# H3 and MLP in two layers: taps packed with k, unit-wise rows for k, v and filter, 39 idle matmuls for 52, and another order list

## The chip, the cores and the metric

The kernel runs on one core of a Trainium2 chip. The metric is the time of one execution on the device in microseconds (us). TensorE (PE) multiplies matrices, VectorE (DVE) and ScalarE (ACT) work element by element, GpSimd (POOL) does little here, and SyncE (SP) issues most DMA transfers; ScalarE issues a few at the start.

## The reference

`x` has 2048 rows of 640 numbers. Two layers are applied twice, A, B, A, B, each on a layer norm of x and added to x:

```python
def A(q, k, v, shift_k, ssm_k, ssm_D):      # q = layernorm(x)
    k_shift = causal_conv(k, shift_k)        # 4 taps a channel
    kv = k_shift * v
    y = long_causal_conv(kv, ssm_k)          # filter as long as the sequence, by FFT
    return q * (y + kv * ssm_D)

def B(x, w1, w2):                            # x = layernorm(x)
    return relu(x @ w1) @ w2                 # 640 -> 1728 -> 640
```

k, v, taps, filter and D are the same in both A layers, so the long convolution is computed once.

## The kernel before

**Tiling.** The 2048 rows are cut into 8 chunks of 256 (`NC`), the 640 channels into 5 tiles of 128 (`NDT`). The long convolution works by units: a unit is one or two (chunk, channel tile) pairs. Chunks 0 and 1 have the units (c,0)+(c,1), (c,2)+(c,3) and (c,4) each; from chunk 2 on most units pair two chunks of one tile. A unit passes through `transform` (L447 on): its k is shifted and scaled by the four taps and summed into `acc` (ScalarE or VectorE), multiplied by v, folded into `sd`; TensorE transposes `sd` into `pt`, ScalarE copies that to `sh`, and TensorE multiplies it by the matrices cM into `pr`, the spectrum `at`. The filter `hf` (for chunk 0 with D added to its first row, L494) is multiplied by the matrices cG and cX into `pg`, the spectrum `gt`. `products` multiplies spectra of all pairs of chunks that meet, sums them on VectorE and turns them back on TensorE (`pq`, with cM). The MLP (`main`) multiplies in float16 in a high and a low part, w1 first (tile `h`), then w2 (tile `o`); its weights `ws` are loaded and split on the chip.

**Order.** Every piece of work is recorded as an operation of one engine, with what it reads and writes (`Plan.op`). The operations are then issued in an order that is written out by hand into the file as text: `ORDER` decodes to 16-bit numbers, each the place of an operation in the order of recording. Every engine executes its own operations in that order, and waits at the first whose inputs aren't there. A buffer of a ring is reused once its last reader is done.

**Start.** 42 idle matmuls (`spin`, L1585, 128x128, identity by identity, read by nobody) are recorded before the first unit and 10 more (L1605) that wait for the first unit's `pg` (6) or `pt` (4). The names in `ACTQ` are fetched on ScalarE's queue: dD, shs (the taps, 10 KB), cG, cX, cM; all else on SyncE's. In the order list ScalarE's start is dD, shs, cG, cX, a first activation (L384), the activation of k's second half (L538), cM. SyncE's is hf, the two pieces of the first unit's k (L471), v, then k, v and hf of the second unit. The first unit multiplies k's first half by taps on VectorE (L540, L545) and starts its second half on ScalarE (L538). On TensorE the list has 42 idle matmuls, four pg operations of the first unit, 6 idle, pt, 4 idle, three pg operations of the second unit, two pr, a pg. A pg operation of a unit of two pairs is four records of 256 columns in the trace.

**Layout.** k, v and the filter lie in memory as [channel tile, chunk, 128 channels, columns] with 262 or 256 float32 columns, so a unit of two pairs is loaded in two rows of 1 KB a partition (`pieces`, L417). The lines that the change touches: `NSPIN`, `NLONG`, `NMORE`, `NLAST` and `ACTQ` (L40), `pieces` (L417), the loads in `transform` (L463 to L475), the first unit's taps (L533 to L547).

Of the kernel before, what the change touches and what calls it, by code (L numbers as in the profile page):

```python
# [18 lines left out]
ALU = mybir.AluOpType  # L19
# [20 lines left out]
NSPIN, NLONG, NMORE, NLAST = 30, 12, 6, 4  # L40
ACTQ = ("cG", "dD", "shs", "cX", "cM")
# [32 lines left out]
    "kO7hbXab7@zX5#$zyWCj!2!Yne*%00W&)A|YXYnSKmx-7)d8*oX9C0l*a2(;#R2*O`vGbK*#U3@`~h(SfCAb9Z30#S{Q-Ugi~`&N"
    "-T`s~+X4Oo;{bsI00NBybOHealmg!Y;Q^5X;sIp<f&$$E;{o6Sa{{megaQHrZUX250|EpB<pJUVbpq)DvI2zy<pKo)Zvy54=K+%f"
    "<N=QY{{e#nh63&Z1_J5<^8l{`cLJ3HkOFoB2LcHK>j9er3Ic}$3j&D(hyw2c@B#4wmI9Xom;wv}>;Z}bz5?w5@&TO!tpc0^=K?hZ"
    "2m-+Zu>$h}nF6x{^Z}j%ngX8!paS&)4FaPAqyiHHr2-BDv;xEep#l#A5CZlA#R9bgrvmo@5dyaY_yM>AK>`v26auCKwgR~V83M)v"
    "LIM>6r~*R*76PdP8Uh~z^8&g8#{$3tL;^SjMFJZFM*^Y(7XrKjAOiIQIt0Q3$O69t=mNU}$pX^?NCHU$7y?QHAp$-G3Ix3ZO9J--"
    "90J1v)B@H5$^y#*B?8w1%mPdT<^m!D=>qBk9Rk$?>;fJF4FvcC*aA%gC;}-0P68$ZCj!v|%>p9=*#h(eECMY8Py#Lj(gJt_Q3Cb?"
    ">jEzV+5-6kFapj3H3BvQ`T{Wm3<OdF?E=pN?gIM)`~o=yI|Tm%+XDRpHUuOB&;r~7?*j1xDgrA4GXgRK76UW_4g?PbIRZBXHv$j@"  # L80
    "{sI64cLW0iQvx~y1OpNT@B#q?7X#e_-U2uR5d=I00s|NW1q0v$6$BFmP6Xcq;Q}KBc?1RnsscL#83XbH2LluY;sQMc7z7#v76d#3"
    "Jpvm8PXr4D7X%~(CIou~J^~p88U!2z9Rno<Cj=q`2m?U`2?HYoKLiQ`8w4N&9s?f(Ap;}>C<7@2<N_Q7OaxE_B?B%4Ap|A^3j-$u"
    "3<DwrF#{b0C<H(RG6M|*LIf%U4g)I$D+7E4F9UuALj*+xDFj9YDg+(`QUrPgQv^5zIRhUAO$1Z~4+D4vFat&cIs-ccECVeAAOtl7"
    "HUmTie+1(KHv=;RGy_otR|H1{J_A(*Rs<3QECekCJOe!gE(8z*KLUaTPXb5;NdsC0Nd#L2KLdmW6ax_hSOlB|69Y;FF9a|ISp-}J"
    "fCNGVN&{sCKm#!ZW(2DOXarpZO9M;;UIbqRnFM_VV+271Lj#)xO#?CnO9W&Dp9F;jp#*~jL<2<wfdo$jPy=TKX#{Nq%miQrP6HJK"
# [36 lines left out]
    "o(dxg?+AGcBnc=9DG4SCTMF<9QVQ`1@(5iDehQrmR0>=QObK2JO$jdvp9-J~P6<y5p$aMqcM2y7#tKjgQ3;|7D+zrHe+pF!EeXjA"
    "dkRtsED2KyR0*RBd<x47Rti`NE(tLSRS8)MG6_}*R|$a%GYOaqS_yy(qzW_%f(rTyUkWz~H3>EeUI|<Yg9?NSFbP`;stQ*M&I(-#"
# [1616 lines left out]
```

## Time and profile before

| | us |
|---|---|
| median of 3 runs | 837.17 |
| lowest and highest | 836.2, 837.32 |
| the profiled execution | 835.64 |
| its span, first to last instruction | 833.9 |
| TensorE busy in it | 828.1 |
| VectorE busy | 776.0 |
| ScalarE busy | 603.7 |

The span is a little shorter than the execution's time, which has a start and an end around it. Times in the trace count from the span's start. PE is a matmul, PEld the load of its weights, which runs beside the matmul before it. A matmul of float32 operands stands in the trace as two records.

### The profile page before, as it was taken

How to read it: one execution, taken by the hardware profiler on the slowest of the kernel's cores; microseconds unless marked ns; L12 is line 12 of the kernel's file. 1: busy time of each engine (PE TensorE's matmuls, PEld its weight loads, DVE VectorE, ACT ScalarE, POOL GpSimd, SP SyncE). 2: the span in 40 equal slices, each digit the busy share in tenths (PEclk: the TensorE clock that was granted, in tenths of full speed). 3: DMA queues.
4: the chain of work that ended last, by engine and by line, in shares of the span. 5: the costliest groups of instructions: out<-in, count | busy, mean ns of one | idle time of the engine just before them, and what ended most of it. 6: DMA issues, size and time to landing. Idle time of an engine off the chain costs nothing.

```text
span 833.9 us, 20585 instructions
## 1 busy us (share of the span) xinstructions
PE 828.1 (99%) x8091; PEld 657.5 (79%) x8091; DVE 776.0 (93%) x1404; ACT 603.7 (72%) x1505; POOL 45.9 (6%) x58
## 2 busy tenths in 40 slices
PE   9999999999999999999999999999999999999998
PEld 8887878887877777777777777777767788888886
DVE  7999999999899999999999999999989799897776
ACT  5997798568997787868668675777736587868532
POOL 0000000000000121000110010111100000000000
PEclk9999999999999999999999999999999999999999
DMA  9978778978999886997997797788997465240300
GB/s 290 385 251 318 266 216 257 278 242 273 315 291 219 263 160 253 258 305 219 235 294 204 211 279 196 231 199 251 306 268 248 140 221 128 64 90 2 58 34 32
DMA packets 138435, 182.37 MB, mean 219 GB/s; under 512 B 53857, under 2 KB 95713, under 8 KB 138338
## 3 DMA queue, kind: packets, MB, share of 16 engines
q1 hardware_dynamic: 129296, 169.60, 65.4%
q0 software_dynamic: 8320, 10.49, 8.5%
q8 instruction: 63, 1.03, 0.5%
q10 hardware_dynamic: 722, 0.96, 0.4%
q14 instruction: 34, 0.28, 0.1%
HBM read 125.24 MB, written 34.08 MB: 191 GB/s over the span
## 4 chain that ended last, share of the span: by engine, by line
PE 99%; POOL 0%; DVE 0%; issue 0%; DVEq 0%; POOLq 0%
PE h L1340 10%; PE h L1343 10%; PE h L1341 10%; PE o L1258 10%; PE o L1313 9%; PE o L1312 9%; PE o L1315 8%; PE h L1328 4%; PE oc L1312 2%; PE oc L1313 2%; PE h L1330 2%; PE oc L1315 2%; PE pg L594 2%; PE hs L1373 2%; PE h L1373 2%; PE pq L816 1%
## 5 line engine op out<-in xcount | busy, mean ns | idle before, releaser
L1343 PE MATMUL h<-xT,w 128*128 128x256 f16 (+1 forms) x1000 | 229.0, 249 | 0.0
L1341 PE MATMUL h<-xT,w 128*128 128x256 f16 (+1 forms) x1000 | 229.0, 249 | 0.0
L1340 PE MATMUL h<-xT,w 128*128 128x256 f16 (+1 forms) x1000 | 229.0, 249 | 0.0
L1313 PE MATMUL o<-w,hh 128*128 128x512 f16 x336 | 127.3, 379 | 0.0
L1312 PE MATMUL o<-w,hh 128*128 128x512 f16 x336 | 127.3, 379 | 0.0
L775 DVE TENSOR_TENSOR pacc<-pacc,pd 128x1536 f32<-128x1536 f32 (+1 forms) x75 | 123.4, 1645 | 0.2
L1341 PEld LDWEIGHTS <-w 128*128 128x128 f16 x1100 | 107.6, 98 | 14.6
L1340 PEld LDWEIGHTS <-w 128*128 128x128 f16 x1100 | 107.6, 98 | 13.6
L1343 PEld LDWEIGHTS <-w 128*128 128x128 f16 x1000 | 97.8, 98 | 6.4
L1313 PEld LDWEIGHTS <-hh 128*128 128x128 f16 x672 | 65.7, 98 | 26.1
L1312 PEld LDWEIGHTS <-hh 128*128 128x128 f16 x672 | 65.7, 98 | 25.8
L770 DVE TENSOR_TENSOR pd<-Ax,Gx 128x768 f32<-128x768 f32 x83 | 78.6, 952 | 1.4 <-DMA Gx<-G 1.2
L1315 PE MATMUL o<-w,hl 128*128 128x512 f16 x208 | 78.8, 379 | 0.0
L1479 ACT ACTIVATE hh<-h 128x512 f16<-128x512 f32 (+1 forms) x97 | 46.7, 483 | 37.6 <-PE h L1328 12.7
L1313 PE MATMUL oc<-w,hh 128*128 128x128 f16 x336 | 73.5, 219 | 0.0
L1312 PE MATMUL oc<-w,hh 128*128 128x128 f16 x336 | 73.5, 219 | 0.0
L1315 PEld LDWEIGHTS <-hl 128*128 128x128 f16 x416 | 40.7, 98 | 24.5
L1328 PE MATMUL h<-xT,w 128*128 128x256 f16 (+1 forms) x400 | 57.8, 251 | 0.0
L1315 PE MATMUL oc<-w,hl 128*128 128x128 f16 x208 | 45.5, 219 | 0.0
L488 ACT ACTIVATE tp<-kt,shs 128x256 f32<-128x256 f32 (+1 forms) x78 | 43.2, 573 | 1.2 <-DVE acc L562 1.0
L770 DVE TENSOR_TENSOR pd<-at,Gx 128x768 f32<-128x768 f32 x46 | 43.1, 952 | 0.1
L1328 PEld LDWEIGHTS <-w 128*128 128x128 f16 x400 | 36.3, 98 | 5.4
(304 smaller groups left out, 2062.1 us busy)
## 6 DMA issues: line engine op xcount, KB each, us to landing
Ax<-A SPq DMA_DIRECT2D x89, 384.0 KB, 5.2
Gx<-G SPq DMA_DIRECT2D x89, 384.0 KB, 4.9
A<-at SPq DMA_DIRECT2D x14, 768.0 KB, 6.1
G<-gt SPq DMA_DIRECT2D x14, 768.0 KB, 6.7
ws<-in_w SPq DMA_DIRECT2D x28, 320.0 KB, 6.5
y<-Y SPq DMA_DIRECT2D x22, 320.0 KB, 4.8
x<-in_q SPq DMA_DIRECT2D x16, 320.0 KB, 4.2
gs<-in_hF SPq DMA_DIRECT2D x20, 256.0 KB, 4.5
```

Source lines behind the costliest of these rows:

```text
L488: ACT.activation(o[:, i : i + m], kview(i, m, j), AF.Copy, scale=shs[:, t, j : j + 1])
L770: ew(f"mac{j % POOLMOD}", 768, lambda e, x=dst[i], av=av, gv=gv: e.tensor_mul(x.t, av(), gv()), [ax, gx], [dst[i]], pr_)
L775: dve(768 * (hi - lo), lambda lo=lo, hi=hi, pd=pd: DVE.tensor_add(acc[:, lo:hi], acc[:, lo:hi], pd[:, lo:hi]), [*sums[lo:hi], *dst[lo:hi]] ...
L1258: PE.matmul(b[:, c : c + w], x, y[:, z : z + w], start=done[i] == 1, stop=end, skip_group_check=fin)
L1312: PE.matmul(z, hh[:, c], wh[:, d], start=(j == JS[0] and i == 0 and (h == 0 or s == S[0])), stop=False)
L1313: PE.matmul(z, hh[:, c], wl[:, d], start=False, stop=end and tail)
L1315: PE.matmul(z, hl[:, c], wh[:, d], start=False, stop=end)
L1328: PE.matmul(p[:, z], wh, xv(t, x), start=b and x == 0, stop=e and x == 1)
L1340: PE.matmul(p[:, z], wh, xv(t, 0), start=b, stop=False)
L1341: PE.matmul(p[:, z], wh, xv(t, 1), start=False, stop=tail and e)
L1343: PE.matmul(p[:, z], wl, xv(t, 0), start=False, stop=e)
L1479: act(2 * R, lambda pv_=pv_, hh=hh: ACT.activation(hh.t, pv_(), AF.Relu), [src], [hh], URGENT)
```

## The change

The taps no longer have a transfer of their own: the array for the first unit's k is 20 columns wider, and its first piece brings taps and k's first half in one DMA. The first unit reads its taps from there; GpSimd copies them to `shs` for the later units. k, v and filter are packed on the host by unit, [unit, 128, 2 x columns], so that a unit of two pairs is one row of 2 KB a partition. Idle matmuls: 34 + 5 in place of 42 + 10. The order list is another one. Decoded and matched to the operations, it starts so: on TensorE 27 idle matmuls, two pg of the first unit, 2 idle, a pg, 3 idle, a pg, 5 idle, pt, 2 idle, three pg of the second unit, two pr, a pg. On ScalarE: dD, cG, cX, the first activation, cM, L538. SyncE's first eight transfers keep their order.

```diff
-NSPIN, NLONG, NMORE, NLAST = 30, 12, 6, 4
-ACTQ = ("cG", "dD", "shs", "cX", "cM")
+NSPIN, NLONG, NMORE, NLAST = 30, 4, 3, 2
+ACTQ = ("cG", "dD", "cX", "cM")
+KW = 262
...
 ORDER = (
...
+SHW = 4 * NDT
...
-    fetch("shs", 80, lambda e: e.dma_start(shs.t, shk), [shs], soonest("shs"))
...
     def pieces(u, ap):
-        (c0, t0), n = u[0], len(u)
-        if n == 1:
-            return ap[t0, c0 : c0 + 1].rearrange("c p n -> p c n")
-        if u[1][1] == t0:
-            return ap[t0, c0 : c0 + 2].rearrange("c p n -> p c n")
-        return ap[t0 : t0 + 2, c0].rearrange("c p n -> p c n")
+        n, z = len(u), SHW if rank(u) == 0 and ap is kT else 0
+        wd = KW if ap is kT else 2 * P
+        return ap[rank(u), :, z : z + n * wd].rearrange("p (c n) -> p c n", n=wd)
...
-            x = R(k, [P, n, wd], k + nm)
+            if (u[0], k) != ((0, 0), "kt"):
+                x = R(k, [P, n, wd], k + nm)
             if u[0] == (0, 0) and k == "kt":
-                kts = [Sub(x, lambda t, i=i: t[:, i]) for i in range(n)]
-                for i in range(n):
-                    dma(4 * wd, lambda i=i: SP.dma_start(kts[i].t, src_kt(u[i])), [], [kts[i]], soonest("kt0_0" + "b" * i))
+                pl, tag, bufs, stream = ring[k]
+                raw = T(pl, tag, bufs, [P, SHW + n * KW], k + nm, stream=stream)
+                x = Sub(raw, lambda t: t[:, SHW:].rearrange("p (c n) -> p c n", n=KW))
+                kts = [Sub(raw, lambda t, i=i: t[:, SHW + i * KW : SHW + i * KW + KW]) for i in range(n)]
+                sh0 = Sub(raw, lambda t: t[:, 0:SHW].rearrange("p (t j) -> p t j", j=4))
+                for i, (z0, z1) in enumerate(((0, SHW + KW), (SHW + KW, SHW + 2 * KW))):
+                    dma(4 * (z1 - z0), lambda z0=z0, z1=z1: SP.dma_start(raw[:, z0:z1], kT[0, :, z0:z1]), [], [kts[i]] + [sh0] * (i == 0), soonest("kt0_0" + "b" * i))
+                plan.op("POOL", 0.2, lambda: POOL.tensor_copy(shs.t, sh0.t), [sh0], [shs], pr_)
...
-                    act(256, lambda i=i, t=t: ACT.activation(accs[i].t, kview(i, 1, 0), AF.Copy, scale=shs[:, t, 0:1]), [kts[i], shs, warm], [accs[i]], pr_, 0.09)
+                    act(256, lambda i=i, t=t: ACT.activation(accs[i].t, kview(i, 1, 0), AF.Copy, scale=sh0[:, t, 0:1]), [kts[i], sh0, warm], [accs[i]], pr_, 0.09)
...
+def _packed(x, more=0):
+    units, wd = _units(), x.shape[3]
+    r = np.zeros((len(units), P, 2 * wd + more), np.float32)
+    for k, u in enumerate(units):
+        for i, (c, t) in enumerate(u):
+            r[k, :, i * wd : i * wd + wd] = x[t, c]
+    return r
...
+    kT = _packed(dl(kl), SHW)
+    kT[0] = np.concatenate([f(A_shift_k).reshape(NDT, P, 4).transpose(1, 0, 2).reshape(P, SHW), kT[0, :, : 2 * KW]], 1)
...
-        "vT": dl(vl),
-        "shk": f(A_shift_k).reshape(NDT, P, 4).transpose(1, 0, 2),
-        "hF": hf.reshape(NDT, NC, P, 2 * P),
-        "hR": hr.reshape(NDT, NC, P, 2 * P),
+        "kT": kT,
+        "vT": _packed(dl(vl)),
+        "hF": _packed(hf.reshape(NDT, NC, P, 2 * P)),
+        "hR": _packed(hr.reshape(NDT, NC, P, 2 * P)),
```

## Rows read from the trace of the kernel before

**Rows 1.** Page, part 1: busy us (share of span), instructions by engine.

```profile
PE 828.1 (99%) x8091; PEld 657.5 (79%) x8091; DVE 776.0 (93%) x1404; ACT 603.7 (72%) x1505; POOL 45.9 (6%) x58
```

**Rows 2.** The page, part 4: the chain that ended last, by engine.

```profile
PE 99%; POOL 0%; DVE 0%; issue 0%; DVEq 0%; POOLq 0%
```

**Rows 3.** Waits of TensorE: who waited for whom, us in total, times, longest us.

```profile
PE spin L1585 <- POOL heps L368: 1.9, 1, 1.9
```

**Rows 4.** Windows: stretch, length, busy us by engine, clock, DMA share, GB/s.

```profile
4.00:6.00 2.00, 2.00 (x22) 2.00 (x20) 1.86 (x5) 0.16 (x1) 0.00 (x0) 1.00 0.95 275
...
20.00:200.00 180.00, 180.00 (x2061) 147.11 (x2060) 176.13 (x348) 141.81 (x357) 0.00 (x0) 1.00 0.86 282
```

**Rows 5.** Chain in order of time, 0 to 24: start us, us, what.

```profile
1.95 4.47 PE spin L1585 x42
6.42 3.51 PE pg L594 x16
9.93 0.34 PE spin L1605 x6
10.26 0.44 PE pt L650 x4
...
10.93 2.84 PE pg L594 x12
```

**Rows 6.** Instructions in order of time around 6 us.

```profile
6.25 0.43 PE L594 MATMUL pg<-hf,cG 128*128 128x256 f32 x1
```

**Rows 7.** ScalarE's queue in order of time; landing time of cG, issued at 1.71.

```profile
1.31 0.36 ACTq L379 DMA_DIRECT2D shs<-in_shk  x1
1.71 0.44 ACTq L388 DMA_DIRECT2D cG<-in_cG  x1
...
6.36 0.33 ACTq L388 DMA_DIRECT2D cM<-in_cM  x1
...
DMA to landing us min/median/max: 4.3/4.3/4.3
```

**Rows 8.** SyncE's queue: landing of first hf, second hf, k's second piece.

```profile
DMA to landing us min/median/max: 2.9/2.9/2.9
...
4.05 0.72 SPq L474 DMA_DIRECT2D hf<-in_hF  x1
...
DMA to landing us min/median/max: 6.4/6.4/6.4
...
L471 SPq DMA_DIRECT2D kt<-in_kT x1: 424/424/424, 1.8 to 1.8; - x1
...
DMA to landing us min/median/max: 4.5/4.5/4.5
```

**Rows 9.** VectorE, ScalarE in order of time: start, us [idle before <-releaser].

```profile
3.72 0.41 DVE L494 TENSOR_TENSOR hf<-hf,dDs 1x256 f32<-1x256 f32 x1 [3.72 <-DMA hf<-in_hF]
...
6.34 0.51 ACT L538 ACTIVATE acc<-kt,shs 128x256 f32<-128x256 f32 x1 [2.18 <-DMA kt<-in_kT]
...
9.51 0.42 DVE L571 TENSOR_TENSOR sd<-acc 128x256 f32<-128x256 f32 x1
10.44 0.41 DVE L494 TENSOR_TENSOR hf<-hf,dDs 1x256 f32<-1x256 f32 x1 [0.52 <-DMA hf<-in_hF]
```

**Rows 10.** GpSimd: a copy, and the page's busy tenths in 40 slices.

```profile
2.26 0.23 POOL L361 COPY down<-ident 64x64 f16<-64x64 f16 x1
...
POOL 0000000000000121000110010111100000000000
```

**Rows 11.** VectorE and TensorE around the pq at 503: start, us, engine, line.

```profile
500.85 0.75 DVE L414 SCALAR_TENSOR_TENSOR hlu<-u,zu,hlu 128x512 f16<-128x512 f32 x1
...
503.15 0.27 PE L392 MATMUL pq<-hlu,cM 128*128 128x256 f16 x1
```

**Rows 12.** Chain in order of time, the end: start us, us, what.

```profile
821.83 8.20 PE o L1258 x74
...
830.12 0.42 DVE x L1546
```

More of the change, by code (lines that the diff above doesn't have):

```diff
@@ new lines @@
+    "_W%F^vjCz1qX3!!0s*uD`2e~A`v9Q;Q~-YfqyPi~oB*2u1_2NOxByiERsj6~5&^0J6alsX76E<$7y+FCR{+-l8UY*ug8;bz9s#8Q"
+    "{{R62*#Lw9g#g$9!vNX<rU0h^+W@Hm0|6ib-2kWn!~om?-T<ut<Nyc(#Q+5X2LY}C2>~Jj3IPiN-vEXH5dp6N-~izO3;`1X$N;?n"
+    "umH&b4FL`T4*}=^=>RkV>HzBiOaV0k#sD?}H~~Qc$^bV3BmqqUCIL<XIRWJWPXQ<a%K$<FIsrQYDgjUdJpoYxz5r4I6#*9k839BA"
+    "KLI`gKmp?b8vz{w9|0i&h5=LoRRKc*BLPJL;s8?tMgfNbRsmN5f&hpCi2;fMivd^xSpg*hCjpEBDFIpmCjct}ECE{qM*+J4jRB4U"
+    "N&zhaE&-1LF99$CF#$*ck^xHrTmfAHUIAYLU;#%0lL3?gya1R1nE{XikpY?kl>uV`VF9@Tx&gZZvH)fQVgbAXn*n42X8~maXaT(e"
@@ new lines @@
+    "zW`|gzX8VpzyZJjmI0RmY5~3hYyoQl!2zBDNdmzD!T@do!U0bLO#(^+%m7FN!vW3!!~tyqp8;<H%>Zx#YyxosoB_!J&j2z3O9G(*"
+    "tN?NWGXZn~&;ZH-fdF#>Oae{<paG%*odKl*ZURsO(ExS<(g0Edbpbp9cLAsYcma6<rU9n`sR4lkdI6&Wqyc*Y(*RQf<^b#g#Q~}T"
+    "d;xv|Q3BKes{vI4RswJWTLOIne*vxmR03@RfB~-otN}9uR|0_n#sPu>tpTzDSOQ!ET>`5Begd!ou>petgaL&C#{pRaZvwLcS^~5I"
+    "wE@ThUIKCgwgJllw*j95Ujobl&jE!3xB=|}?g60!U;=RhNdaR5?*Y*P%>mE>WCCRZqXO^&SO9YZ@d3^O)B$t?^8wWX(g9}z^Z|7O"
+    ")&biAgaX_FhXQ~C(*a=u*a7tcW&(Et=K$3J<^p&E_5s!a_W_0i*8$l9b^`bTf&yX!Xac1Ig93R1+5w;f-2veNhyvmP-vQVH`2mgs"
@@ new lines @@
+    "+5&$9i2~jM-~nm^`T_g_X#)KL{sD>tivoHAd;+2Z<pJga{{gWAkOF%Gj{@TXi~{5VkpiRwk^++g=K<&erUJAA@&SzkeFC@w00IF5"
+    "lmeClvjUd_C<LbhC;;gJr~(E8w*smHx&i_M0|M#+m;$Q;ngRy`=mH1=1Ol=G1p=7@sRFD5xdNL4oB|92>j5+ZD+HASH3BvQtpW)G"
+    "4FU=REd)0LF$59<`vJQGuL89K69PB_t^zs&yaL+-3j(kL#sUrk{R2A!JOVue6aqd1>H-e}wgSfjy#mPsz5*Bm$^yRvKLXhT6$0D>"
+    "-2xB-$O7L25dr`N>jKLH8v;NA90C~vK>`{A!~(zq76Qxy9|GqBAOb@IAp*q$YXU?9=>pyYA_C0<>;fYKC<4I(DFW>RBm(~fMFQXg"
+    "!UEv}?gH-uECenD@&e8R@B%3W7Xrfq&jR8C9RlP69s(u;B?2b`0R#dBECLAwDg-J5@d5(`^8#uF_5wx%Eduuf;{pW)^a9WV3Iovs"
@@ new lines @@
+    "D*^-rF9h`h3j_E9(*g(t1_aUqK?KwS76fbr`2w8+E&>b#<pTNw)dB|uFa!$(4FfL%2?Q_#4g*32{sRgG7X%puZUiv`3<M7Y4FnJa"
+    "7z7#w6$ASMGz9zt76UQ_{Q?dI5d#wg5(5+i7Xupu90S(^4+K91Lj)KD6a*my83X<T8Uz0V6$B&$5Cj_pGXy0AH3R?y9RnT%0RtWc"
+    "Zv-L(aRfF5I0PI7IRqU95d=j9Z3G_!AOkA{ECWUa5(Gd5M+5=`YXl<$IRY&ME(0h769g#(Hw1D7)&eF2Dg!42L<C9%NCZg)Is`ET"
+    "1p^-hF9RS1Fase30|PPwbp%2JI|MufO$0myP6RRocLWCm1OrP1j|2t-Jp>{IBLqwYPXu!WH3K~ZSOhZzBm`Lmo&sA0J_Aq$KLb$&"
+    "QUr_ya0FHaGy^sRjs!phB?LYMR|Jv-cm$LLHv@JAI0HfhbOb{KS_E7KU<AJeQv^W+2m?d|c?3lR!30PHIRjJ#Is-`qP6NXPl?0On"
@@ new lines @@
+    "RRop<VFX44mjrqQM*~U&T?E7gngmM&kOX1`R0Ep?Oaop7R|8`NSOa7Pm;{*wRRenjPXl}ejRc$oeFU8ZRs((nPy<Z^e*{|tQ3HSk"
+    "Uj)VkqXfkSWdvLUQUiemQv+TDCj^27o&<vgT?1wWqy)zV$OOOyWCNcBkpx)-Wdm9RHw7jHg#@4kh6JSq$^^^=rUYLDW&>aYgapC_"
+    "X9LLuVFQN*KLw`*Km}?AZv&zOIt8c%hy<wwVgon@a06!qaRYS&Jq11mp#(Vv%>;=AiUf88ssy40V*{-OXalPRasz1ta|1yIiv+9$"
+    "cLS~j%LI4>&IIWLuLREoumoxY&;&vSLj`LC(FA(~(gb`1(*$e<bOW^nu>^esYy;s0fdg#=f&;b$ZUcD(g9Ca4I|Y6NZUv(QvIJ-Z"
+    "w**B6vjo%xZv}({L<NTfqyt6;r32LjiUWuPxCEvHM+Ha)i36tta0RIY)&$oCe*<v^Nd>9{I|Ggbivw~6a|M6{g#*|Gh69WPj{{Bx"
@@ new lines @@
+    "jRQ&rs{@e(lLcu6kOR5|l>@8;v;?gKYXz<YJO!5n+63DKuLF_;Z3T4&m;<l_vIE%!xdfI2b_I6@O9glZlLOoYvjda^;{=-nnFCM-"
+    "Q3Z4bQU#g=y99X!dIjACoC8w@R0W*_PX(R>v;(yRRRvZBl?8kSwgXHBSOvTTyae6^p96jcpaaGQoCQ|}<piMvw*$BX-vn6&eFeD#"
+    "$OXLvn+56vx&!M2S_QiU>;vrsz5~JozXQMndj-e??gQ`xr~}CZ!2??b!vpaH@&l9w$_1ST$^-KQe+8Ze%LBv%U<Jzs#RK#M^#jfW"
+    "O$ELL%mwxX_XE!Z(F4!}#skL#%mbhW(gV!}fCbe9&IS1cfd!TY%>!Ho)&tlB*8}1Ny#(Y0(FNxOVFl&{p9T5@Vg=I!-UHtQ=mcE_"
+    "-~-_U*#nma`vcko+XLwY>ICZq>;&!vUIo+x?*yR*+ymVM&jsKFUj^a=`~%Vj1O?**<O8Aw@dV`qs0CvM@C0N9m<6!|<^!1png!Ga"
@@ L163 @@
+    "c@KvVi4S@YYY%%5iVuhngAaTUeGh^U;0}Keiw}$skq>?kjSr3wfDeTah7W`fk`I#)l@F8;mJg2)n-7o=nGc!|mk*y0m=B^4oDZN6"
+    "p%0@Erw^nLr4OhNoe!oDo)4-IsSm6Vtq-dYt`Dyd"
 )
@@ L199, with _units @@
 ONPOOL = ()
+SHW = 4 * NDT
+def _units():
+    units = []
+    for c in range(2):
+        units += [[(c, 0), (c, 1)], [(c, 2), (c, 3)], [(c, 4)]]
+    for c in range(2, NC, 2):
+        m = NDT - 2 * SPLIT[c // 2 - 1]
+        units += [[(c, t), (c + 1, t)] for t in range(m)]
+        units += [[(e, t), (e, t + 1)] for e in (c, c + 1) for t in range(m, NDT, 2)]
+    return units
 def fview(ap):
@@ L295, in tile_h3_mlp @@
 @with_exitstack
-def tile_h3_mlp(ctx: ExitStack, tc: tile.TileContext, q, kT, vT, shk, hF, hR, dD, w1, w2, cM, cG, cMh, cGh, out):
+def tile_h3_mlp(ctx: ExitStack, tc: tile.TileContext, q, kT, vT, hF, hR, dD, w1, w2, cM, cG, cMh, cGh, out):
     nc = tc.nc
@@ L544, in f @@
                     def f(i=i, t=t, j=j):
-                        DVE.scalar_tensor_tensor(accs[i].t, kview(i, 1, j), shs[:, t, j : j + 1], accs[i].t, op0=ALU.mult, op1=ALU.add)
-                    dve(256, f, [kts[i], shs, accs[i]], [accs[i]], pr_, 0.13)
+                        DVE.scalar_tensor_tensor(accs[i].t, kview(i, 1, j), sh0[:, t, j : j + 1], accs[i].t, op0=ALU.mult, op1=ALU.add)
+                    dve(256, f, [kts[i], sh0, accs[i]], [accs[i]], pr_, 0.13)
         else:
@@ L696, in transform @@
         return at, gt, lambda: (sums(), sum_a(), spill())
-    src_kt = lambda p: kT[p[1], p[0]]
-    units = []
+    units = _units()
     def rank(u):
@@ L1591, in tile_h3_mlp @@
         dma(512 * k, lambda t=t, x=x: SP.dma_start(t.t, x), [], [t], LATER)
-    for c in range(2):
-        units += [[(c, 0), (c, 1)], [(c, 2), (c, 3)], [(c, 4)]]
-    for c in range(2, NC, 2):
-        m = NDT - 2 * SPLIT[c // 2 - 1]
-        units += [[(c, t), (c + 1, t)] for t in range(m)]
-        units += [[(e, t), (e, t + 1)] for e in (c, c + 1) for t in range(m, NDT, 2)]
     both = (0, 1)
```

173 lines of the change are left out of this document (70 added, 103 removed).

## The prediction, made before the changed kernel was timed

> **What bounds the kernel now.** I read the page's busy times first: TensorE is busy 828.1 of 833.9 us, VectorE 776.0, ScalarE 603.7 [rows 1]. Then the chain that ended last: 99% of it is TensorE [rows 2], and the list of TensorE's waits holds one, 1.9 us before its first instruction [rows 3]. So the end is TensorE's own work laid end to end; an edit counts only if it changes that work, leaves the engine idle, or moves its start or the tail. The windows say the same of the body: 180.00 of 180 us busy from 20 to 200, with VectorE at 176.13 beside it [rows 4]. VectorE is the engine that would next be late.
>
> The chain in order of time [rows 5] shows where TensorE does nothing useful. 42 idle matmuls (spin) take 4.47 us from 1.95, then come 16 records of pg, 6 idle matmuls (0.34), pt, 4 idle ones, and a group of 12 pg in 2.84 us. 16 pg took 3.51, or 0.219 each, so 12 are worth 2.63 and 0.21 us is a stall; VectorE's rows name it: the add of dD to the second hf ran at 10.44, after waiting for that hf's DMA [rows 9].
>
> The two kinds of idle matmul are the same 128-column instruction: 4.47/42 = 0.106 us early and 0.34/6 = 0.057 later. 128 columns in 0.106 us is TensorE's 1.2 GHz level, in 0.057 its 2.4 GHz level. The granted clock printed for 4 to 6 us is 1.00 [rows 4], but the pace there is half, so I go by the pace. From 1.95 to the first pg at 6.25 [rows 6] there are 4.30 us for 42 instructions, 0.17 less than 4.47; at 0.050 saved on each fast one that is 3.4 fast ones, so the clock rose at about 6.06, some 4.1 us after TensorE began.
>
> Outside the span lie 835.64 - 833.9 = 1.74 us, which I leave alone. The profiled execution is 1.53 us below the median of the runs shown (837.17; lowest 836.2). I work out a difference against 835.64 and carry it to the median. Less than 0.2% (1.67 us) can't be told from no change.
>
> **The change part by part.** I laid the new order list over the old one entry by entry. TensorE's 963 entries that aren't idle are the same set; 595 keep their place among themselves, 368 move, and the last 169, from 720.3 us on, are in the old order. So the tail (the last 74 matmuls, then VectorE and the store [rows 12]) is taken as it is.
>
> *Start.* Before the first pg stand 27 idle matmuls instead of 42. They end at 1.95 + 27 x 0.106 = 4.82. The first pg waits for hf with dD added (3.72 + 0.41 = 4.13 [rows 9]) and for cG. cG was issued at 1.71 and took 4.3 us to land [rows 7], at 6.01; pg followed 0.24 later. Now the shs transfer, issued ahead of it at 1.31 [rows 7], is gone, and cG takes its place, 0.40 us earlier. With the same time to land pg starts at 5.85. Ends: 4.82 (cG lands as quickly as the first hf, 256 KB in 2.9 us [rows 8], that is at 4.2) and 6.25 (landing is set by bytes, not by the issue). I take 5.85, nearest to cG's own row. Until 6.06 pg runs at 1.2 GHz, which loses half of 0.21, or 0.11. Net gain here 0.29.
>
> *Idle matmuls after the first pg.* The new list puts 2 after the first two pg entries, 3 and 2 around the next two, 3 before pt and 2 after: 12, where there were 10. At 0.057 that costs 0.11. So of the 13 that are gone none is saved here; the saving is the earlier start.
>
> *pt and the second pg.* pt needs sd, whose VectorE chain hangs on the second piece of k (ScalarE's L538 waited 2.18 us for it, to 6.34), and sd ended at 9.51 + 0.42 = 9.93 [rows 9]; pt ran right behind. The chain, which counts a matmul from the end of the one before, has pt at 10.26 [rows 5]; with the new start TensorE comes to it at 6.42 - 0.40 + 0.11 + 3.51 + 10 x 0.057 = 10.21, so it and sd still arrive together and pt gains less than 0.1. After pt (0.44) and 2 idle matmuls (0.11) the second unit's pg can start at 10.76, where it started at 10.93, if the second hf and its add are there. The add can't begin before sd ends (9.93) and so ends at 10.34 at the earliest; before it ended at 10.85. Which one holds depends on when that hf lands: it was issued at 4.05 and took 6.4 us [rows 8]. Its rows are now twice as long; but cM, 384 KB, issued at 6.36 behind L538 [rows 7], now stands ahead of L538 and shares the engines earlier. From both sides: gain 0 here (hf at 10.4 again) to 0.4 (hf before 9.9; then PE's own work is the limit, and the 0.21 stall is gone too). I take 0.3: the terms above, 0.29 - 0.11, with half of the 0.21 stall recovered.
>
> *The k, v and filter layout.* Rows of 2 KB instead of two of 1 KB. The nearest rows lie far apart: cG, 256 KB in 2 KB rows, landed in 4.3 us, the second hf, 256 KB in 1 KB rows, in 6.4 [rows 7, 8], under different loads. So a load lands between 2.1 us earlier and no earlier. Cover: TensorE waits for nothing after its start [rows 3], so past 11 us this is worth nothing; within it, it is part of the ends above. Without that cover (a load that arrives last) a filter landing late stalls pg by its delay.
>
> *Taps.* They come with k's first piece, 10 KB more on 131 KB. A GpSimd copy writes shs for the later units. Nearest row: a copy of 64x64 in 0.23 us [rows 10]; behind it on GpSimd nothing runs for hundreds of us, as the engine's slices show [rows 10], and the first reader of shs is the second unit's taps, behind L538 at 6.34 [rows 9]. Ends: 0 and 0.2; I take 0.
>
> *The rest of the list.* With every operand ready when it was in the trace, ten TensorE entries would now be asked for before their last input, by up to 1.75 us. The worst is the pq at 503.15, asked for 3.3 us earlier; its last input, a VectorE split, ran at 500.85 for 0.75 [rows 11], 1.55 us before it. But the list also takes 11 VectorE instructions, 8.9 us, out from ahead of that split. I followed six of the ten: each has more work taken from ahead of its input than it lacks. I take 0; ends 0 and 1.75 (a later stall covers an earlier one, so they don't add).
>
> Sum: 835.64 - 0.3 = 835.3 for the profiled execution; 837.17 - 0.3 = 836.9 for the median. Its own range, by the gains 0 to 0.4 and the scatter of the runs shown (836.2 to 837.32), is 835.8 to 837.4.
>
> **Rivals.**
> *Nothing changes (the queue earlier, the bytes not).* cG and the second piece of k landed 0.3 us apart (1.71 + 4.3 = 6.0 and 1.8 + 4.5 = 6.3 [rows 7, 8]), as transfers that share something do. If cG gains what k loses, sd ends up to 0.4 later and the gain goes: 837.1 to 837.3. The Trainium skill (DMA: Bandwidth & Descriptors, "Issuing engines are not separate DMA queues") says just that: DMAs of ScalarE and SyncE run on the same 16 engines and interleave. The two landings agree with it.
>
> *Slower: the clock rises late.* TensorE now idles from 4.82 to 5.85, in the stretch that led to the rise at 6.06. For: in the trace it worked without a break for 4.1 us before the rise. Against: it still works 2.9 of the 3.9 us before pg. If the 4.1 us count from pg instead, the clock stays at 1.2 GHz until 9.96, and 4.11/2 = 2.06 us of work is lost where the forecast loses 0.11: 2.06 - 0.11 - 0.3 = 1.65 slower, 838.8 (837.17 + 1.65). It decides for "slower" once the low level lasts beyond 9.96. The Trainium skill (TensorE: Matmul & The Clock Gate, "What's actually happening") says that the throttled clock is the default, that activity releases it, and that the monitor's watch does not begin with the kernel, so the moment varies between runs. No row here shows how it takes a break; by that page the same program could also rise early or late by chance.
>
> *Slower: the list stalls TensorE.* If the pq at 503.15 gets nothing from VectorE's new order, 1.75 is lost: 837.17 + 1.75 = 838.9. Against: the 8.9 us taken out ahead of its input.
>
> *Faster.* cG lands at 4.6 or before, pg starts at 4.82, 1.43 earlier, of which half of 1.24 is lost to the low clock, and the second hf is early too: 0.8 at most, since sd holds pt. That is 836.4; the median falls below 835.5 only if the runs also lie as low against it as the profiled one did.
>
> **How the numbers follow.** Forecast 0.48; nothing changes 0.12; late clock 0.16, of which 0.09 over the bound, since its price sits on it; list stall 0.12, of which 0.08 over it; faster 0.12. Faster by over 0.2% (below 835.5): 0.12. Slower (above 838.84): 0.09 + 0.08 = 0.17. Within: 0.48 + 0.12 + 0.07 + 0.04 = 0.71. The range takes in the rivals' prices: 835.2 to 839.0.
>
> **What would show it.** Right: 39 spin, the first pg at 5.6 to 6.0 and cG issued at 1.3; pg of the second unit at 10.5 to 10.9; TensorE's waits still one or two short ones; the last matmul 0.3 earlier. Wrong: spin or pg at 0.106 and 0.43 us a piece beyond 7 us (the clock); a wait of TensorE over 0.5 us anywhere after 20 us (the list); pt later than 10.3 (k's second piece lost what cG gained). A change of over 1.7 us in a stretch where the PE's list is the old one would be none of these, and the prediction would be wrong in kind.

## The result and the profile after

The changed kernel takes 840.58 us (median of 5 runs, 840.19 to 841.93) against 837.17 (836.2 to 837.97) for the kernel before on the same chip: ratio 1.0050, 95% interval 1.0039 to 1.0061. That is slower, and outside the range that was given. The profiled execution took 841.16 us.

The page of the changed kernel, three lines of it (the span; part 1, busy time; part 4, the chain that ended last by engine), against [rows 1, 2]:

```profile
span 839.4 us, 20572 instructions
PE 829.4 (99%) x8078; PEld 657.1 (78%) x8078; DVE 775.9 (92%) x1404; ACT 603.3 (72%) x1505; POOL 46.3 (6%) x59
PE 87%; DMA 4%; DVE 4%; issue 1%; ACT 1%; SPq 1%; POOL 0%; DVEq 0%; POOLq 0%; ACTq 0%
```

The work is the same: 13 matmuls fewer, VectorE and ScalarE within 0.4 us of before. The chain, all TensorE's before [rows 2], now runs through other engines. The waits of TensorE say where; before there was one, ahead of its first instruction [rows 3] (columns: who waited for whom, us in total, times, longest us).

```profile
PE pnu L419 <- ACT pnu L417: 2.6, 1, 2.6
PE spin L1601 <- POOL epst L381: 1.9, 1, 1.9
PE pr L407 <- DVE hla L428: 0.7, 1, 0.7
PE pg L407 <- DVE hlg L428: 0.5, 1, 0.5
PE h L1344 <- DMA xT<-xh: 0.4, 1, 0.4
PE pg L636 <- DVE ys L870: 0.2, 1, 0.2
```

Names that are new here: ScalarE squares and sums a tile, and TensorE adds the sums up in pnu, pna or png, which gives the scale for a split; hlu, hla, hlg, and hh with hl in the MLP, are such splits into a high and a low float16 part, the low one made by VectorE; xh is a layer-normed piece of x, which a transposing transfer turns into xT, the input of h; hb and oc are further sums of the MLP; pd and pacc are VectorE's products and their sums.

I laid the two traces side by side at points up to which both lists hold the same entries. TensorE of the changed kernel is 1.20 us ahead at its 253 us, 0.30 ahead at 327 us and 5.80 behind at 727 us, from where the lists agree. So the start gained, and the stretch from 253 to 727 us lost 7.0 us in this execution. Of these, 4.2 us are the four waits above from 0.4 us on, and 1.65 us a stretch at half pace behind the longest, which is shown below; these rows do not locate the last 1.1 us or so.

The start, from the chain in order of time (start us, us, what), against [rows 5]:

```profile
1.95 3.01 PE spin L1601 x27
4.96 1.78 PE pg L611 x8
9.13 0.45 PE pt L667 x4
9.69 2.65 PE pg L611 x12
```

ScalarE and VectorE in order of time (start, us), the multiplication of k's second half and the end of sd, against 6.34 and 9.51 before [rows 9]:

```profile
5.44 0.51 ACT L555 ACTIVATE acc<-kt 128x256 f32<-128x256 f32 x1 [1.78 <-DMA kt<-in_kT]
8.61 0.42 DVE L588 TENSOR_TENSOR sd<-acc 128x256 f32<-128x256 f32 x1
```

cG landed 3.3 us after its issue at 1.30, not 4.3, so pg followed the 27th idle matmul at once. The first 8 pg have 0.22 us a record, which is full pace: here the clock rose before 5 us.

The largest wait, on ScalarE in order of time (start, us, instruction, in brackets the idle time before it and what ended it):

```profile
438.58 0.59 ACT L417 ACTIVATE pnu<-u 128x512 f32<-128x512 f32 x1
443.82 0.63 ACT L526 ACTIVATE hr<-hr 128x512 f32<-128x512 f32 x1 [4.53 <-DMA gs<-hr]
444.36 0.58 ACT L417 ACTIVATE pnu<-u 128x512 f32<-128x512 f32 x1
```

The negation of hr (L526) may overwrite hr only when the accumulating transfer that reads it is done; ScalarE stood 4.53 us in front of it, and behind it in the queue stood the second half of the square that TensorE's pnu needs. In the old list the negation stands ten places behind that square, in the new one three places ahead of it (places in the list of all engines). The kernel before has the same wait where it harms nobody (its line L509, with what ended the engine's idle time):

```profile
L509 ACT ACTIVATE hr<-hr x2: 622/626/630, 409.2 to 441.4; 128x512 f32<-128x512 f32 x2
  DMA gs<-hr: 1.7, 1
```

Behind the wait TensorE ran at its lower clock level, as windows of the changed kernel show (stretch, length, busy us by engine with counts, granted clock, DMA share, GB/s):

```profile
440.00:442.50 2.50, 2.50 (x21) 1.56 (x19) 2.50 (x4) 0.00 (x0) 0.00 (x0) 1.00 1.11 286
445.20:448.30 3.10, 3.10 (x17) 2.20 (x17) 1.49 (x4) 3.07 (x11) 0.51 (x1) 0.50 1.07 333
448.30:452.00 3.70, 3.70 (x30) 2.20 (x28) 3.16 (x6) 2.65 (x8) 0.00 (x0) 0.97 0.30 53
```

0.50 is 1.2 GHz. By the starts of the matmuls against their spacing at full pace, this stretch loses 1.65 us beside the wait, which by the same count is 2.77 us long (the list above, which goes by modelled ends, has 2.6).

One more late entry, on SyncE (start, us of issuing, instruction): four transposing transfers of xT, the last issued at 615.60, though its input was ready at 609.62:

```profile
608.52 1.21 SPq L1207 DMA_TRANSPOSE xT<-xh  x1
610.45 2.06 SPq L1207 DMA_TRANSPOSE xT<-xh  x1
613.23 1.21 SPq L1207 DMA_TRANSPOSE xT<-xh  x1
615.60 2.02 SPq L1207 DMA_TRANSPOSE xT<-xh  x1
```

The old list issues that transfer second of the four; in the trace of before all four are issued by 609.3.

### The profile page after: what moved, and what is told of

Same layout as the page of the kernel before. It is cut to its first block, busy times and chain, and to the rows that moved or that the text cites. A ratio compares the mean times of both kernels' runs of the same rounds, so it can differ in the third digit from the quotient of the medians.

```text
span 839.4 us, 20572 instructions
## 1 busy us (share of the span) xinstructions
PE 829.4 (99%) x8078; PEld 657.1 (78%) x8078; DVE 775.9 (92%) x1404; ACT 603.3 (72%) x1505; POOL 46.3 (6%) x59
## 2 busy tenths in 40 slices
DMA packets 127667, 182.37 MB, mean 217 GB/s; under 512 B 53713, under 2 KB 74321, under 8 KB 127570
## 4 chain that ended last, share of the span: by engine, by line
PE 87%; DMA 4%; DVE 4%; issue 1%; ACT 1%; SPq 1%; POOL 0%; DVEq 0%; POOLq 0%; ACTq 0%
PE o L1274 10%; PE h L1356 9%; PE h L1359 9%; PE h L1357 9%; PE o L1329 7%; PE o L1328 7%; PE o L1331 7%; PE h L1344 4%; PE oc L1328 2%; PE pg L611 2%; PE oc L1329 2%; PE h L1346 2%; PE hs L1389 2%; PE h L1389 2%; PE oc L1331 2%
## 5 line engine op out<-in xcount | busy, mean ns | idle before, releaser
L1357 PEld LDWEIGHTS <-w 128*128 128x128 f16 x1100 | 107.9, 98 | 14.7
L1356 PEld LDWEIGHTS <-w 128*128 128x128 f16 x1100 | 107.9, 98 | 14.0
L1359 PEld LDWEIGHTS <-w 128*128 128x128 f16 x1000 | 97.8, 98 | 6.3
L527 POOL DMA_DIRECT2D gs<-hr x20 | 19.1, 957 | 412.7 <-DVE pacc L791 219.5
```

What stands on the lines that cost most here:

```text
L1356: PE.matmul(p[:, z], wh, xv(t, 0), start=b, stop=False)
L1357: PE.matmul(p[:, z], wh, xv(t, 1), start=False, stop=tail and e)
L1359: PE.matmul(p[:, z], wl, xv(t, 0), start=False, stop=e)
```

## The experiments

N is the new list decoded, O the old one with its entries renumbered, and k is N where single entries are moved; unless said otherwise all else of the change is in. The edits are shown in this short form: where N or O is edited, the text of `ORDER` in the kernel holds the result. Ratios are to the kernel before on the same chip, with 95% intervals. The expectations of experiments 2 and 5 to 7 speak of theories M and S, which are set out at the end of experiment 3.

**1. The old list.**

```diff
-order = N
+order = O
```

> Everything of the change but the order list: rows by unit, taps with k, 39 idle matmuls (34 of them before the first pg), the list of before with its entries renumbered. Theory A (all of the loss is in the list): no TensorE wait over 0.3 us after the first pg, and 836.2 to 837.4, since the transfers at the start land earlier and 8 fewer idle matmuls stand before pg (gain 0 to 1.0 against before). Rival (the layout slows the transfers, so that entries that were in time in the old list are late): stalls at 320 to 340 or 440 us with the old list too, 839 to 841.

836.50 us (12 runs), 0.9991 [0.9981, 1.0002]. The layout, the taps and the number of idle matmuls cost nothing that shows; the list costs 1.0050/0.9991 = 0.59%, 4.9 us. That settles the cause in the large. The rest of the forecast (0.3 us faster, or 0.9996) lies inside the interval. TensorE's waits in this trace:

```profile
PE hb L1356 <- DVE hl L1496: 0.7, 1, 0.7
PE h L1356 <- DVE hl L1496: 0.5, 1, 0.5
```

So the old list has small waits too, in some executions, where I had expected none over 0.3. Its chain is 84% TensorE's, less than the changed kernel's 87%, at 4 us less: the shares of the chain show which engine was last, not what it cost.

**2. The new list in parts.**

```diff
-order = N
+order = N[:1460] + O[1460:]
```

> The change with the new list for its first 1460 entries (TensorE to 253 us) and the old order behind that; both lists hold the same set of entries up to there. By the two traces the new list stands 1.20 us ahead of the old one at that point. Theory A: that lead is kept to the end, 835.5 to 836.5, below both kernels. Rival B (the lead makes an input late that was just in time, and is given back): 836.8 to 837.6. Rival C (the loss comes with the layout): 839 or more.

836.85 (12 runs), 0.9998 [0.9988, 1.0008]. The time is rival B's: the lead of 1.20 us isn't there. But no input needs to have given it back: in this trace the clock rose late, 8 pg took 3.27 us where they took 1.78 above, and the second unit's pg began at 11.23, so there was no lead to keep.

```profile
1.94 3.06 PE spin L1601 x27
5.01 3.27 PE pg L611 x8
11.23 2.65 PE pg L611 x12
```

```diff
-order = N
+order = N[:1780] + O[1780:]
```

> The change with the new list for its first 1780 entries (TensorE to 327 us), the old order behind them. Theory M (between 327 and 724 us the new list asks TensorE's entries too close behind their inputs, so transfers that land a little later in one run than in another stall it there, at other entries in each run): what is lost is lost behind 327 us, so 836.4 to 838.0 here, with at most 1 us of waits before 327 us (pg near 325). Rival S (a few fixed entries cost it, pg near 325 among them): 837.6 to 838.6, with pg near 325 and pr near 335 waiting again.

```diff
-order = N
+order = O[:1780] + N[1780:]
```

> The counterpart: the old order for the first 1780 entries, the new list behind them. Theory M: the loss is all here, 839.2 to 841.0, with two or more waits of TensorE over 0.5 us between 327 and 724 us. Rival S (VectorE's wait at 320 us, in the new list's earlier part, starts the later stalls): 836.5 to 838.5.

The new list up to 327 us: 837.82 (12 runs), 1.0017 [1.0007, 1.0027]. From 327 us on: 838.21 (12 runs), 1.0015 [1.0005, 1.0026]. I had put all of the loss behind 327 us, and that was wrong. Against the old list's 0.9991 the stretches cost 0.07% to 253 us, 0.19% from there to 327, 0.24% behind: 0.50 of the 0.59%. Each ratio is known to 0.1% only, so the first of these can't be told from nothing; the loss is spread over at least the other two.

**3. One entry moved: the negation of hr behind the square of pnu.**

```diff
+        k.insert(2275, k.pop(2268))
```

> The new list with one ScalarE entry moved seven places back: the negation of hr (unit 6_1), which waited 4.5 us for an accumulating transfer, now stands behind the square of pnu (unit 4_4) that was queued behind it. Theory A (the new list lost its time where an in-order engine waits for an accumulating transfer and TensorE's input stands behind it; after a wait of 2.7 us TensorE ran some 3 us at half pace): the 2.6 us wait of pnu and the half pace around 445 to 448 us both go, up to 4.6 us in the profiled execution, so 836.0 to 838.0 where the new list gave 840.58, and TensorE's waits keep only pr 0.7 and pg 0.5. Rival B (VectorE and ScalarE are simply behind in this list from 320 us on, and this entry is only where it shows): the wait of TensorE comes back within 20 us at another entry, and the time stays within 1 us of 840.6. Rival C (the low clock near 445 us is not caused by the wait): the wait goes and a stretch of half pace stays; 838.0 to 839.0.

840.97 (6 runs), 1.0046 [1.0029, 1.0063]: no gain that shows, against up to 4.6 us expected. The wait of pnu and the half pace behind it are gone, as theory A said, but TensorE then came earlier to entries that were no earlier, pq near 450 us, as rival B had it, and h near 618 us. Its largest waits now:

```profile
PE h L1346 <- DMA xT<-xh: 1.8, 1, 1.8
PE pq L409 <- DVE hlu L430: 0.7, 1, 0.7
PE pr L409 <- DVE hla L430: 0.6, 1, 0.6
```

Theory A fell here, and I went on with two: S, a few single entries each cost their wait, and M, the list leaves TensorE too little margin everywhere, so a wait that is taken away comes back at the next entry.

**4. One entry moved: a pd that waits for a transfer, behind the splits on VectorE.**

```diff
+        k.insert(1774, k.pop(1753))
```

> The new list with one VectorE entry moved 21 places back: the pd of unit 4_1 that waited 2.1 us at 319.7 us for the transfer of at now stands behind the splits hl and hlg that were queued behind it. Theory A (that one wait puts VectorE behind, and the stalls of pg near 325 us, 0.5 to 0.9, and of pr near 336 us, 0.7 to 0.9, both come from it): both go, 1.7 us less, 838.4 to 839.3, with the 2.6 us wait of pnu still there. Rival B (VectorE has too much work in that stretch whatever its order): pr near 336 us still waits over 0.5 us; 839.6 to 840.8.

839.55 (12 runs), 1.0031 [1.0020, 1.0043]: of the single moves in the new list the only one that gained, 1.0 us by the medians and 1.6 by the ratios. The pr wait is gone and pg's at 325 us too. Other waits stand in their place, h near 618 us with half pace behind it:

```profile
PE h L1346 <- DMA xT<-xh: 2.1, 1, 2.1
PE pnu L421 <- ACT pnu L419: 1.2, 1, 1.2
```

**5. Both moves, and the changed kernel again beside them.**

```diff
+        k.insert(2275, k.pop(2268))
+        k.insert(1774, k.pop(1753))
```

> The new list with both entries moved: the negation of hr behind the square of pnu, and the pd of unit 4_1 behind the splits. Theory M: the waits at 325, 335 and 442 us go and others come, above all h near 618 us for the transposing transfer of xT (1.9 and 2.1 us with either move alone): 838.5 to 840.0. Rival S (these entries were the cause): 836.0 to 837.5.

> The changed kernel as it is, on the same chip as the runs beside it, for a second trace. Theory M: 839.6 to 841.5, and the waits of TensorE are not the ones of the first trace: pnu near 442 us differs by over 1 us from 2.6, h near 618 us by over 0.5 from 0.4, and their sum is again over 4 us. Rival S: pnu 2.6, pr 0.7 and pg 0.5 again, within 0.3 each. The clock's rise at the start, if it is by chance, puts the second unit's pg anywhere from 9.7 to 11.2 us.

Both moves: 838.88 (12 runs), 1.0029 [1.0018, 1.0040], as theory M had it, with these waits in place of those at 325, 335 and 442 us:

```profile
PE h L1347 <- DMA xT<-xh: 2.2, 1, 2.2
PE pq L410 <- DVE hlu L431: 1.4, 1, 1.4
```

The changed kernel again: 841.34 (6 runs), 1.0060 [1.0039, 1.0081]. Its second trace has other sizes than the first, and again over 4 us in all:

```profile
PE h L1344 <- DMA xT<-xh: 1.6, 1, 1.6
PE pnu L419 <- ACT pnu L417: 0.9, 1, 0.9
PE pg L407 <- DVE hlg L428: 0.8, 2, 0.5
PE pna L419 <- ACT pna L417: 0.7, 1, 0.7
PE pr L407 <- DVE hla L428: 0.7, 1, 0.7
```

The places recur, the sizes don't: pnu had 2.6 and 0.9, h 0.4 and 1.6. In these two traces the larger the one, the later TensorE comes to the other, and the less is left of it.

**6. The late xT transfer: mended in the new list, made late in the old one.**

```diff
+        k.insert(2275, k.pop(2268))
+        k.insert(1774, k.pop(1753))
+        k.insert(2969, k.pop(2993))
```

> The new list with three entries moved: the negation of hr and the pd of unit 4_1 as in the run with both moves (838.88), and the second transposing transfer of xT, which the new list issues last of four on SyncE, 6 us after its input is ready (609.6, issued 615.6 in the first trace), issued second as in the old list. Theory S (few fixed entries cost it, and this is the largest): the wait of h near 618 us (0.4 to 2.2 in every trace of the new list's later part) goes, with the half pace behind it where the wait was over 2 us; 1.7 to 4 us less than with both moves, 835.5 to 837.2, and TensorE's waits hold only pieces under 1 us. Theory M (the margin is short everywhere, so the next input is late instead): under 1 us less, 838.0 to 838.9, with a wait over 1 us elsewhere between 600 and 724 us.

```diff
+        k.insert(2969, k.pop(2993))
```

> The new list with the xT transfer alone moved to its old place, second of four. Theory S for this entry: the wait of h near 618 us goes (0.4 to 2.2 in the traces, at times with half pace behind it), and the time is 1 to 3 us below the changed kernel's 840.6 to 841.3: 838.0 to 839.8, with the waits of pnu near 442 us and pr near 335 us still there. Theory M: less than 1 us.

Three moves: 837.95 (12 runs), 1.0011 [0.9998, 1.0024], 0.9 us below both moves, a step that the two intervals do not quite separate. The h wait at 618 is gone, and no wait over 1 us came in its place, though theory M had expected one; left in its trace are pq and another h:

```profile
PE pq L411 <- DVE hlu L432: 1.0, 1, 1.0
PE h L1360 <- DVE hl L1508: 0.8, 1, 0.8
```

The same entry moved alone: 841.00 (5 runs), 1.0056 [1.0041, 1.0071], nothing, though its wait is gone there too: pnu waited 2.6 us before it. Here a wait mended behind a larger one showed no gain, as did a larger one mended ahead of the next (experiment 3). The three single moves change the ratio by -0.04, -0.19 and +0.06 points, all three together by -0.39: together they were worth more than singly, as far as intervals of 0.1 to 0.2 points show it.

```diff
-order = O
+O.remove(2593); O.remove(3034); i = O.index(3243); O[i:i] = [3034, 2593]
+order = O
```

> The old list in the new layout (836.5 alone) with one change: that transposing transfer of xT is issued behind four loads of Ax and Gx that followed the transposes, some 6 us later. Theory S: this one entry makes TensorE wait at h, by 2 to 4 us; where the wait is over 2 us TensorE runs at half pace for some 3 us behind it and loses 1.6 to 1.7 more; nothing makes up for it, since TensorE is the bound to the end: 838.5 to 842. Theory M (a single late input is absorbed or shifts other waits away): 836.3 to 837.5.

838.77 (12 runs), 1.0025 [1.0009, 1.0042], 2.3 us above the old list, in theory S's range. No half pace followed the wait of h:

```profile
PE h L1344 <- DMA xT<-xh: 1.9, 1, 1.9
```

So one late entry, in a list whose other waits are small, costs about its whole wait.

**7. Two more moves, and two in the old list.**

```diff
+        for x, y in ((2646, 2235), (2648, 2235), (3055, 3270), (3057, 3270)):
+            k.remove(x)
+            k.insert(k.index(y) + 1, x)
```

> The new list with the three moves and two more on VectorE: a pd and a pacc behind the two splits hlu that pq waits for near 450 us, and two pd behind the split hl that h waits for near 647 us (waits of 1.0 and 0.8 us in the trace with three moves, 837.95). Theory S (single late entries, each paid by its wait): both waits go, 1 to 2 us less, 836.0 to 837.2, no more than 0.3% from the kernel before on either side. Theory M (the margin is short, what is moved back is late in its turn): 837.5 to 838.5, with new waits of 0.5 us or more between 440 and 724 us.

```diff
-order = O
+for x, y in ((2756, 2388), (2749, 2388), (2217, 2283)):
+    O.remove(x); O.insert(O.index(y) + 1, x)
+order = O
```

> All of the change but its list (836.5 with the old list as it was), the old list with the splits hl near 421 and 492 us ahead of the pd instructions that stood before them (waits of 0.5 and 0.7 us there). If these two waits are in most runs, 0.5 to 1.2 us less, 835.2 to 836.0, below both kernels; if the pd behind them are needed as soon, the waits move on and 836.2 to 837.0.

Five moves: 839.25 (6 runs), 1.0037 [1.0025, 1.0049]. Both waits are gone, and pnu near 656 us waits 1.2: theory M in kind, though the time is above its range, and not below three moves. The old list with two splits earlier: 836.84 (12 runs), 1.0000 [0.9991, 1.0010]. Those waits went and one of 0.9 came at 512 us. No version was below both kernels beyond the noise; the lowest is the change with the old list.

**8. What standing still does to the clock.** The late transfer of experiment 6, first with 48 idle matmuls in its wait, then made later by one more load, without and with idle matmuls (60 and 118 in place of the 48).

```diff
+            if o.seq == 3243:
+                self.idle(self.ops[3248].new[0])   # 48 matmuls of 128 columns
             o.fn()
```

> The run with the late transfer, and 48 idle matmuls of 128 columns (2.6 us at full pace) just ahead of the matmul that waits for it, so that TensorE works through most of the wait. If the half pace behind long waits comes from the engine having stood still: no matmul at half pace behind the wait, and 0.8 to 1.7 us less than the late transfer alone. If it comes from something else (the transfer, the chip): the half pace stays, and the time is the same within 0.5 or up to 1 us more, if the idle matmuls outlast the wait.

```diff
-O[i:i] = [3034, 2593]
+O.remove(3036); i = O.index(3243); O[i:i] = [3034, 3036, 2593]
```

> The old list with the transposing transfer of xT behind one load more than in the run where it was late (838.77; there the wait was 1.9 us and no half pace followed). The wait of h is now 3 to 4.5 us, longer than the 2.26 to 2.77 behind which half pace was seen: some 3 us at half pace follow, so besides the wait 1.6 to 1.7 us are lost: 841 to 843. If half pace had another cause: 839.5 to 841.

> The same with 60 idle matmuls of 128 columns (3.2 us at full pace) just ahead of the matmul that waits. If TensorE's standing still brings the half pace, none follows, and the time is 1.2 to 1.7 us below the run without them; if not, it is the same within 0.5 us.

> The old list with the much later transfer of xT (844.28; wait 6.3 us, then 16 matmuls at half pace worth 1.65), and 118 idle matmuls (6.3 us at full pace) ahead of the matmul that waits, so that at most some 1 us of standing still is left. If standing still brings the half pace: no stretch at half pace after 620 us, and 1.0 to 1.7 us less, 842.6 to 843.4. If not: the half pace is there, or the time is 844 or more.

With 48 idle matmuls: 839.04 (11 runs), 1.0024 [1.0014, 1.0034], like the late transfer alone; there was no half pace to save, so it decides nothing. The later transfer: 844.28 (4 runs), 1.0095 [1.0082, 1.0108]; h waited 6.3 us, not the 3 to 4.5 expected, and half pace followed. With 60 idle matmuls: 845.91 (4 runs), 1.0111 [1.0096, 1.0125]; 3.2 us of waiting were left, and half pace followed again. The waits of these two traces (the second names a load of Gx, but the transposing transfer, issued at 617.17 and 6.5 us on its way, landed as h began):

```profile
PE h L1344 <- DMA xT<-xh: 6.3, 1, 6.3
PE h L1346 <- DMA Gx<-G: 3.2, 1, 3.2
```

845.91 is 1.6 us above the run without idle matmuls, which neither side of the expectation had; the profiled execution, the lowest of the four runs at 844.29, doesn't show why. With 118: 844.12 (5 runs), 1.0101 [1.0084, 1.0119], with no wait of this h and no half pace. Windows of the second and the fourth kernel:

```profile
618.00:624.90 6.90, 0.57 (x4) 0.17 (x3) 3.56 (x6) 1.26 (x4) 1.19 (x1) 0.74 0.99 266
624.90:628.00 3.10, 3.10 (x15) 2.19 (x15) 0.00 (x0) 0.00 (x0) 0.00 (x0) 0.50 0.64 251
```

```profile
618.00:624.90 6.90, 6.90 (x124) 6.85 (x121) 2.08 (x4) 0.74 (x3) 1.02 (x1) 1.00 1.03 267
624.90:628.00 3.10, 3.10 (x31) 2.78 (x29) 0.56 (x1) 0.60 (x1) 0.00 (x0) 1.00 0.20 79
```

Kept busy, TensorE does 31 matmuls in the 3.10 us in which it did 15 at half clock. The mean granted clock of the timed runs agrees: 0.996 in all four without idle matmuls, 1.0 or 0.999 in the five with 118. So the standing still brings the low clock; in the 6.3 us wait it fell before the wait was over, as the 0.74 of its window shows. The medians gain nothing by it, where 1.0 to 1.7 us were expected. One part is seen: in the trace with 118 idle matmuls the transfer, issued at 618.03, landed 5.6 us later, and h began 0.8 us behind that, when the last idle matmul was done. The rest isn't explained by these traces.

## Why the prediction was wrong

- **First pg at 5.85, net gain 0.29.** The moment was wrong, and the gain hung on something else. I took cG's own landing time, 4.3 us [rows 7]; without the shs transfer it was 3.3 in the first trace, near the low end that I had priced (pg at 4.82). pg began at 4.96 or 5.01 in most traces with 27 idle matmuls. What was then gained hung on the clock, whose rise I had put at 6.06 from one trace; by the pace it came before 5 us in the first trace and near 7.9 us in that of experiment 2: the second unit's pg, forecast for 10.76, came at 9.69 to 11.27 in ten traces with 27 idle matmuls ahead (middle 10.6 to 10.7), and at 9.89 to 10.85 in eight with 34 (middle 10.4 to 10.5). Experiment 2 shows no gain from the new start.
- **12 idle matmuls behind the first pg, 0.11 more than 10.** Right: 0.11 + 0.17 + 0.11 + 0.17 + 0.11 = 0.67 us for 12, against 0.34 + 0.22 = 0.56 for 10 [rows 5].
- **pt not later than 10.3, second pg no longer held.** Right in the first trace (pt at 9.13), but not by the working: sd was to end at 9.93 and hold pt, and it ended at 9.03, since k's second piece was there at 5.44 and not at 6.34. So the second unit's pg came 1.24 us earlier, more than the 0.8 that I had given the rival "faster" at most, and "cG gains what k loses" did not happen: both gained. With the clock late, as in experiment 2, pt came at 10.68.
- **Layout and taps at nothing.** Right, by experiment 1. Packets under 2 KB fell from 95713 to 74321 at the same 182.37 MB, and the time stayed. The kernel before, and the changed one:

```profile
DMA packets 138435, 182.37 MB, mean 219 GB/s; under 512 B 53857, under 2 KB 95713, under 8 KB 138338
DMA packets 127667, 182.37 MB, mean 217 GB/s; under 512 B 53713, under 2 KB 74321, under 8 KB 127570
```

- **"The rest of the list ... I take 0; ends 0 and 1.75."** This is the step that failed; it measured 4.9 us. I compared each TensorE entry's new moment with the moment its last input had been ready in the old trace. But the new list moves ScalarE's, VectorE's and SyncE's entries too, so the inputs themselves come later: the square of pnu stood behind a wait for a transfer, the fourth transpose six us behind its input. The sign that I had named for this, a wait of TensorE over 0.5 us after 20 us, is in the first trace with pnu (2.6) and pr (0.7). The pq at 503.15 that I named worst waited nowhere; from 480 to 560 us the first trace has no wait. I followed six of ten entries, and none of those that waited over 0.4 us in the first trace was among the ten. The old trace held the warning: ScalarE waited 1.7 us at L509 with nothing urgent behind it.
- **"A later stall covers an earlier one, so they don't add."** Half right, and the likely reason why two of the three single repairs in the new list showed no gain. It holds for two neighbours, one of which hides the other; along the whole list they summed to several us: TensorE's waits come to 4.4 us behind its first instruction in the first trace of the changed kernel and, with the small ones that aren't shown, to over 5 in the second.
- **Rivals.** "The list stalls TensorE" (0.12, 838.9) was the right kind at the wrong place and too small. "The clock rises late" was seen in several traces as a difference from run to run of the same start, and isn't what makes the change slower: the traced execution of experiment 2's first kernel has it, at 837.69 us, 2.9 below the changed kernel's median.

What stays open: with three moves 0.2% is left against the old list (1.0011 to 0.9991), and five moves were no better. That is what a short margin on VectorE and ScalarE would do, but it isn't shown entry by entry. Neither theory holds alone: one late entry put into the old list cost its wait, as S has it, while most entries mended in the new list gave way to the next late one, as M has it.

## What to carry to other kernels

When an order written by hand is replaced, it isn't enough to ask whether TensorE's inputs were ready in the old trace: every engine's queue has to be replayed, and the entries to look at first are those that moved ahead of others while they wait for a transfer. A kernel whose TensorE is busy 99% of the time and whose VectorE is at 92% has its time in the margins between them; here a handful of waits of 0.4 to 2.6 us cost more than the edit at the start could give. A repair that removes the largest wait and leaves the time as it was suggests that the next late input was hidden behind it; repair several together before judging.

## What the runs showed that I had not expected

- **Half pace behind waits in mid-kernel.** Waits of 2.1 (experiment 4), 2.2 (experiment 5), 2.6 (first trace, and the xT entry alone in experiment 6), 3.2 and 6.3 us (experiment 8) were each followed by some 3 us at 0.50 of the clock, a loss of 1.5 to 1.7 us each, the same for the long as for the short ones. Behind waits of 1.9 (experiment 6), 1.8 (experiment 3) and 1.6 (experiment 5) there was none. The Trainium skill (TensorE: Matmul & The Clock Gate, "HAM oscillation — how this bites in real kernels") tells of a matmul engine that waits for transfers and starts again at the low clock; these traces agree. It is not the main part of the loss: a mean clock of 0.998, which goes with one such stretch, shows in one of the changed kernel's 11 runs.
- **The clock's rise at the start differs from run to run.** The same instructions ran their first 8 pg in 1.78 to 3.27 us, which alone moves the second unit by up to 1.5 us. A forecast of a few tenths at the start can't be told from that in single traces.
